# Transposes by DMA straight from SBUF, one per token tile, and zero matmuls before the first work, in a fused attention and FFN kernel

## The chip, the cores and the metric

The kernel runs on one core of a Trainium2 chip. The metric is the device time of one execution in microseconds (us). Profiles show one profiled execution; their span runs from the first to the last instruction. The engines in them are PE (TensorE matmuls), PEld (TensorE weight loads), DVE (VectorE), ACT (ScalarE), POOL (GpSimd) and SP (SyncE, which here only issues DMAs; SPq is its queue).

## What is computed

The input x has 2048 tokens of 1024 features. LayerNorm gives xn; a linear attention block (32 heads of 32) and a SwiGLU FFN with hidden size 3584 both work on xn. Cut to what matters:

```python
xn = layernorm(x)
q, k, v = split_heads(xn @ wqkv)                   # 32 heads of 32
phi = lambda t: where(t > 0, t + 1, exp(t)) + 1e-6
kv, z = einsum(phi(k), v), sum(phi(k))             # over all tokens
o = (phi(q) @ kv) / (phi(q) . z + 1e-6)
s = o @ wo
g = silu((silu(xn @ w_gate) * (xn @ w_up)) @ w_down)
out = x + s * g
```

All inputs and the output are bfloat16.

## The kernel before

TensorE multiplies along the partition axis, so it needs xn and o with features on partitions and tokens on the free axis (`xnT`, `oT`), while LayerNorm and the attention's division produce them with tokens on partitions (`xn`, `o_blk`). The 2048 tokens are 16 tiles of 128 (`NT`), in 4 blocks (`NB`) of 4 tiles (`TPB`). Phase 1 goes over the 16 token tiles: LayerNorm, transpose, then four groups (`c` = 0 to 3) of eight matmuls each, two for k and two for v (`emit_Bmm`, evacuated by `emit_Bev`), and the sum over tokens of k times v (`emit_C`, tile `kvz`). Phase 2 makes q, divides (`emit_ND`), transposes o (`emit_OT`) and multiplies by wo (`emit_S`). Phase 3 is the FFN, which uses a Strassen-like scheme with sums of xn (`S`) and of weights (`T`). Engines execute in the order in which the program emits, except where noted.

LayerNorm of tile i: statistics on VectorE, 1/sqrt by Newton steps on small tiles on GpSimd, the normalization on VectorE. Two tiles (0 and 1) take the root from ScalarE instead.

```python
def emit_stats(i):                       # VectorE: bn_stats x2, bn_aggr
    ...
def emit_rstd(gid):
    eng = nc.gpsimd
    ...
    eng.tensor_scalar(out=a[:, 0:n], in0=mv[:, 0:n, 1], scalar1=EPS_LN, scalar2=None, op0=ALU.add)
    nc.vector.tensor_single_scalar(out=yi, ...)          # first guess by the bits
    nc.vector.tensor_scalar(out=yi, ...)
    for _ in range(3):                                   # NR_ITERS
        eng.tensor_tensor(out=w[:, 0:n], in0=y, in1=y, op=ALU.mult)
        eng.tensor_tensor(out=w[:, 0:n], in0=w[:, 0:n], in1=a[:, 0:n], op=ALU.mult)
        eng.tensor_scalar(out=w[:, 0:n], in0=w[:, 0:n], scalar1=-0.5, scalar2=1.5, ...)
        eng.tensor_tensor(out=y, in0=y, in1=w[:, 0:n], op=ALU.mult)
def emit_N(i):                           # VectorE: xn = (x - mean) * rstd
    xn = work.tile([P, D], BF16, name="xn", tag="xn")    # pool of 2
    ...
```

Tiles 0 to 7 are transposed on TensorE, eight 128x128 transposes each, and copied out of PSUM. Tiles 8 to 15 go, four at a time, to DRAM and come back through a transposing DMA:

```python
def emit_TR(i):                          # tiles 0 to 7
    tr_ps = psC.tile([P, dch, P], BF16, name="tr_ps", tag="C")
    for dc in range(dch):
        nc.tensor.transpose(tr_ps[:, dc, :], xn[:, ...], ident[:])
    ...                                  # copy to xnT by VectorE (tiles 0, 1) or ScalarE

def emit_A2_block(b):                    # tiles 8 to 15
    xn_blk = work.tile([P, TPB, D], BF16, name="xn_blk", tag="xn_blk")
    for t in range(TPB):
        emit_norm(b * TPB + t, xn_blk[:, t, :])
    nc.sync.dma_start(out=blk_rows_pt(xn_dram, b), in_=xn_blk[:])
    nc.sync.dma_start_transpose(out=xn_blk_tiles[b][:], in_=blk_rows(xn_dram, b))
```

The evacuation of a k group (`emit_phi`, not in place for the first nine tiles) is two ScalarE passes, exp into `e_t` and relu into `r_t`, and two VectorE passes, which write `pk_sb`. `e_t` and `r_t` have two buffers each, the kv PSUM tiles three. The main loop of phase 1:

```python
for i in range(2, NT):
    for c in range(NCH):                                 # 4
        emit_Bmm(i, c)
        if c == 0:
            if i + 1 < NPE:                              # NPE = 8
                emit_TR(i + 1)
            emit_C(i - 1)
        emit_Bev(i, c)
        ...                                              # norms and statistics of later tiles
    if i == 3 or i == 5:
        wt, wv = (wq_sb, wqkv_v) if i == 3 else (wo_sb, wo_v)
        for c in range(NCC):
            nc.gpsimd.dma_start(out=wt[:, :, c * CW:(c + 1) * CW], in_=wv[:, :, c * CW:(c + 1) * CW])
    if i >= 10:
        prep(1)                                          # weight sums T for the FFN, on GpSimd
```

In phase 2 each half block of o (two token tiles) goes to DRAM and back:

```python
def emit_OT(b, hf):
    ...
    nc.sync.dma_start(out=rows.rearrange("(t p) d -> p t d", p=P), in_=o_blk[:, hf * th:(hf + 1) * th, :])
    nc.sync.dma_start_transpose(out=oT_tiles[b][:, :, hf * tk:(hf + 1) * tk], in_=rows)

def nd_item(b, t):
    def f():
        emit_ND(b, t)
        if t % 2 == 1:
            emit_OT(b, t // 2)
            prep(1)
    return f
```

In the last block the four `emit_ND` stand among the `emit_S` of the block before it; then come the sums `S` for the FFN (`emit_Ssum`, VectorE, into memory that the o blocks have left) and the eight `emit_S` of the last block. The loads of the first FFN weights are held back until the first of those eight begins.

Of the kernel before, what the change touches and what calls it, by code (L numbers as in the profile page):

```python
# [10 lines left out]
ALU = mybir.AluOpType  # L11
# [10 lines left out]
def kernel(  # L22
# [11 lines left out]
    nc = tc.nc  # L34
# [22 lines left out]
    NJ = (G + GPT - 1) // GPT  # L57
    EPS_LN = 1e-5
    EPS = 1e-6
    PE_T_BLOCKS = min(2, NB)  # L60
    NPREP = 12

    wqkv_v = A_wqkv.rearrange("(dc p) n -> p dc n", p=P)
# [41 lines left out]
    def xn_ap(dcs, tok):  # L105
        b = tok.start // TB
        return xn_blk_tiles[b][:, dcs, tok.start - b * TB:tok.stop - b * TB]
# [7 lines left out]
        nc.gpsimd.memset(v_bufs[k][:, :, P:P + 1], 1.0)  # L115
    KVZ = late.tile([P, G, NDW], BF16, name="KVZ")
    s_dram = dram.tile([S, D], BF16, name="s_dram")
    xn_dram = dram.tile([S, D], BF16, name="xn_dram")
    o_dram = dram.tile([S, D], BF16, name="o_dram")
    HK = DC // 2  # L120
    TB2 = 2 * TB
    t_drams = {}

    def blk_rows(t_dram, b):
        return t_dram[b * TB:(b + 1) * TB, :]

    def blk_rows_pt(t_dram, b):
        return t_dram[b * TB:(b + 1) * TB, :].rearrange("(t p) d -> p t d", p=P)

    def emit_phi(work, t_ps, dst, W, in_place=False, act=False):  # L130
        e_t = work.tile([P, W], FP32, name="e_t", tag="e_t")
# [123 lines left out]
    with ExitStack() as p1:  # L255
        wpool = p1.enter_context(tc.tile_pool(name="p1w", bufs=1))
        work = p1.enter_context(tc.tile_pool(name="p1work", bufs=2))
        small = p1.enter_context(tc.tile_pool(name="p1small", bufs=4))

        wkv_sb = wpool.tile([P, DC, 2 * D], BF16, name="wkv_sb")  # L260

# [36 lines left out]
            load_wkv(c)  # L298
        for i in range(nx, NT):
            load_x(i)  # L300
        NPE = min(PE_T_BLOCKS * TPB, NT)
        STAT_AT = {2: (8, 9), 3: (10, 11), 5: (12, 13), 6: (14, 15)}
        FMAX = nc.vector.BN_STATS_FMAX
        SCH = min(FMAX, D)
        NSC = D // SCH
# [4 lines left out]
        grp_state = {}  # L310

        def grp_of(i):
            return i if i < NPE else NPE - PE_T_BLOCKS + i // TPB

        def grp_tiles(gid):
            if gid < NPE:
                return [gid]
            b = gid - NPE + PE_T_BLOCKS
            return list(range(b * TPB, min((b + 1) * TPB, NT)))

        def emit_stats(i):
            gid = grp_of(i)
            if gid not in grp_state:
                mv = small.tile([P, TPB, AGG], FP32, name="mv", tag="mv")
                rstd = small.tile([P, TPB], FP32, name="rstd", tag="rstd")
                grp_state[gid] = (mv, rstd, grp_tiles(gid))
            mv, rstd, tiles = grp_state[gid]
            k = tiles.index(i)
            stats = small.tile([P, NSC, nc.vector.BN_STATS_DIM], FP32, name="stats", tag="stats")
            xr = x_ap(i).rearrange("p (c f) -> p c f", f=SCH)  # L330
            sts = [nc.vector.bn_stats(out=stats[:, c, :], in_=xr[:, c, :]) for c in range(NSC)]
# [13 lines left out]
            nc.vector.reciprocal(out=rstd[:, 0:n], in_=rstd[:, 0:n])  # L345
            return sq

        def emit_rstd(gid):
            eng = nc.gpsimd
            mv, rstd, tiles = grp_state[gid]  # L350
            n = len(tiles)
            a = small.tile([P, TPB], FP32, name="lna", tag="lna")
            eng.tensor_scalar(out=a[:, 0:n], in0=mv[:, 0:n, 1], scalar1=EPS_LN, scalar2=None, op0=ALU.add)
# [12 lines left out]
        def emit_norm(i, dst, cols=None):  # L366
            mv, rstd, k = ln_state[i]
            src = x_ap(i) if cols is None else x_ap(i)[:, cols]
            return nc.vector.tensor_scalar(out=dst, in0=src, scalar1=mv[:, k, 0:1], scalar2=rstd[:, k:k + 1],
                                           op0=ALU.subtract, op1=ALU.mult)  # L370
# [1 line left out]
        xn_tiles = {}  # L372

        def emit_N(i):
            xn = work.tile([P, D], BF16, name="xn", tag="xn")
            xn_tiles[i] = xn
            if i == 0:
                for hh in range(2):
                    cols = slice(hh * (D // 2), (hh + 1) * (D // 2))
                    emit_norm(i, xn[:, cols], cols=cols)  # L380
            else:
                emit_norm(i, xn[:])
            ln_state.pop(i)

        def emit_TR(i):
            tok = slice(i * P, (i + 1) * P)
# [3 lines left out]
            for hh in range(nh):  # L390
# [5 lines left out]
                    nc.vector.tensor_copy(out=dst, in_=tr_ps[:])  # L396
                else:
                    nc.scalar.copy(out=dst, in_=tr_ps[:])

        def emit_A2_block(b):  # L400
            xn_blk = work.tile([P, TPB, D], BF16, name="xn_blk", tag="xn_blk")
            for t in range(TPB):
                emit_norm(b * TPB + t, xn_blk[:, t, :])
                ln_state.pop(b * TPB + t)
            nc.sync.dma_start(out=blk_rows_pt(xn_dram, b), in_=xn_blk[:])
            nc.sync.dma_start_transpose(out=xn_blk_tiles[b][:], in_=blk_rows(xn_dram, b))

        pkv_tiles = {}

# [2 lines left out]
        def emit_Bmm(i, c):  # L412
            tok = slice(i * P, (i + 1) * P)
            kv_ps = psB.tile([P, CW], FP32, name="kv_ps", tag="B")
            kv_banks[(i, c)] = kv_ps
            for dc in range(DC):
                mm = nc.tensor.matmul(kv_ps[:], lhsT=xn_ap(dc, tok), rhs=wkv_sb[:, dc, c * CW:(c + 1) * CW],  # L417
                                      start=(dc == 0), stop=(dc == DC - 1))
                if dc == 0 and c == 0:
                    marks[("B", i)] = mm  # L420
# [23 lines left out]
        def ln_pre(i):  # L444
            emit_stats(i)
            emit_rstd(grp_of(i))

        emit_stats(0)
        emit_rstd_act(0)
        emit_N(0)  # L450
# [3 lines left out]
        emit_N(1)  # L454
        emit_Bmm(0, 0)
        emit_TR(1)
        ln_pre(2)
        emit_Bev(0, 0)
        emit_Bmm(0, 1)
        emit_Bmm(1, 0)  # L460
        emit_Bev(0, 1)
        ln_pre(3)
        emit_Bev(1, 0)
        emit_N(2)
        emit_Bmm(1, 1)
        emit_Bmm(0, 2)
        emit_Bev(1, 1)
        emit_Bev(0, 2)
        emit_Bmm(1, 2)
        emit_Bev(1, 2)  # L470
        ln_pre(4)
        emit_TR(2)
        emit_N(3)
        emit_Bmm(0, 3)
        emit_Bev(0, 3)
        emit_Bmm(1, 3)
# [2 lines left out]
        for i in range(2, NT):  # L479
            for c in range(NCH):  # L480
                emit_Bmm(i, c)
                if c == 0:
                    if i + 1 < NPE:
                        emit_TR(i + 1)
                    emit_C(i - 1)
                emit_Bev(i, c)
                if c == 1:
                    if i + 2 < NPE:
                        emit_N(i + 2)
                    if 5 <= i + 3 < NPE:  # L490
                        ln_pre(i + 3)
                if c == 2:
                    if i in STAT_AT:
                        for k in STAT_AT[i]:
                            emit_stats(k)
                            if k % TPB == TPB - 1:
                                emit_rstd(grp_of(k))
                    if i - 1 in STAT_AT and STAT_AT[i - 1][-1] % TPB == TPB - 1:
                        emit_A2_block(STAT_AT[i - 1][-1] // TPB)
            if i == 3 or i == 5:  # L500
                wt, wv = (wq_sb, wqkv_v) if i == 3 else (wo_sb, wo_v)
                for c in range(NCC):
                    nc.gpsimd.dma_start(out=wt[:, :, c * CW:(c + 1) * CW], in_=wv[:, :, c * CW:(c + 1) * CW])
            if i >= 10:
                prep(1)
        emit_C(NT - 1)
        ps1.close()
# [36 lines left out]
    with ExitStack() as p2:  # L544
# [35 lines left out]
                    in1=rden[:, 0:ng, :, None].to_broadcast([P, ng, HPG, DH]),  # L580
                    op=ALU.mult)

        def emit_OT(b, hf):
            if hf == 0:
                oT_tiles[b] = otp.tile([P, G, TB], BF16, name="oT", tag="oT")
            o_blk = o_blks[b]
            th, tk = TPB // 2, TB // 2
            rows = o_dram[b * TB + hf * tk:b * TB + (hf + 1) * tk, :]
            nc.sync.dma_start(out=rows.rearrange("(t p) d -> p t d", p=P), in_=o_blk[:, hf * th:(hf + 1) * th, :])
            nc.sync.dma_start_transpose(out=oT_tiles[b][:, :, hf * tk:(hf + 1) * tk], in_=rows)  # L590

        def emit_S(b, t, cc):
            oT = oT_tiles[b]
# [20 lines left out]
        def nd_item(b, t):  # L614
            def f():
                emit_ND(b, t)
                if t % 2 == 1:
                    emit_OT(b, t // 2)
                    prep(1)
            return f  # L620

# [239 lines left out]
```

## Time and profile before

| | |
|---|---|
| median of 3 runs | 815.3 us |
| lowest and highest | 811.02, 815.36 us |
| span of the profiled execution | 813.0 us |
| TensorE busy | 792.4 us |
| VectorE, ScalarE, GpSimd busy | 446.0, 236.9, 205.0 us |
| DMA | 178.92 MB, mean 220 GB/s |

Phase 1 lasts until about 135 us, phase 2 until about 261 us, the FFN until the end. In the profile an operation is named by its line, engine, output and inputs; `tr_ps` are the TensorE transposes, `kv_ps` the matmuls for k and v, `kvz` the sum over tokens, `q_ps` and `s_ps` those of phase 2, `yb`, `xb`, `zw`, `y_pd` and `y_ps` the FFN. `a <- b` in a list of waits means that a waited for b. Overlapping matmuls are shown with their whole length through the pipeline, so the rate of a series is read from the length of the series, not from the mean of one.

### The profile page before, as it was taken

To read this page: it belongs to the slowest core of one execution; us is meant where nothing else is said; L and a number is where in the kernel's file an instruction comes from. 1 tells how busy PE (TensorE), PEld (TensorE's weight loads), DVE (VectorE), ACT (ScalarE), POOL (GpSimd) and SP (SyncE) were. 2 spreads that over 40 slices of the span, in tenths; PEclk is the share of its full clock that TensorE was granted. 3 is DMA by queue.
4 is the path that set the end of the run, shared out by engine and by line. 5 is a ranking of instruction groups with operands and counts; after the bars stand their busy time and mean duration, and the time that the engine had idled before them with its cause. 6 is when DMAs were issued, how large, how long until landed. Compare 5 with 4: busy or idle time off the path is not lost.

```text
span 813.0 us, 10086 instructions
## 1 busy us (share of the span) xinstructions
PE 792.4 (97%) x3808; PEld 432.4 (53%) x3808; DVE 446.0 (55%) x700; ACT 236.9 (29%) x388; POOL 205.0 (25%) x309
## 2 busy tenths in 40 slices
PE   6999999999989999999999999999999999999997
PEld 2544444444444666666665444466666666644443
DVE  6676334684544666767765044177667676610405
ACT  4544333866523322222221020032222222200102
POOL 2472695034342253443650010010000000000200
PEclk9999999999998999999999999999999999999999
DMA  9239953079689778778686548489777777753641
GB/s 318 97 135 232 299 215 156 0 228 262 222 255 296 237 228 264 244 232 276 205 302 216 189 137 322 136 275 323 255 258 249 238 251 253 258 195 130 218 144 52
DMA packets 150784, 178.92 MB, mean 220 GB/s; under 512 B 30928, under 2 KB 106064, under 8 KB 150736
## 3 DMA queue, kind: packets, MB, share of 16 engines
q1 hardware_dynamic: 137984, 137.25, 53.7%
q0 software_dynamic: 10304, 36.71, 12.7%
q10 hardware_dynamic: 2448, 4.33, 1.6%
q8 instruction: 30, 0.49, 0.3%
q14 instruction: 18, 0.15, 0.1%
HBM read 127.93 MB, written 44.04 MB: 212 GB/s over the span
## 4 chain that ended last, share of the span: by engine, by line
PE 88%; DMA 5%; DVE 3%; POOL 2%; issue 1%; ACT 1%; SPq 0%; DVEq 0%
PE zw L663 25%; PE xb L663 12%; PE y_pd L748 12%; PE y_ps L748 11%; PE kv_ps L417 8%; PE s_ps L600 7%; PE yb L663 6%; PE q_ps L165 4%; DMA oT<-o_dram 2%; DMA xnT<-xn_dram 1%; DMA xn_dram<-xn_blk 1%; DMA xp<-in_A_x_dram 1%; PE kvz L439 1%; PE nd_ps L569 1%; DVE sy L785 0%
## 5 line engine op out<-in xcount | busy, mean ns | idle before, releaser
L663 PE MATMUL zw<-S,T 128*128 128x512 f32 x672 | 175.3, 409 | 0.0
L748 PEld LDWEIGHTS <-hT 128*128 128x128 bf16 x896 | 87.7, 98 | 105.7
L663 PEld LDWEIGHTS zw<-S,T 128*128 128x128 f32 x672 | 126.4, 188 | 32.3
L417 PE MATMUL kv_ps<-wkv_sb,xnT 128*128 128x512 bf16 x512 | 115.2, 383 | 1.9 <-DMA xnT<-xn_dram 1.8
L663 PE MATMUL xb<-xnT,w_sb 128*128 128x512 bf16 x448 | 115.2, 380 | 0.0
L748 PE MATMUL y_ps<-w_sb,hT 128*128 128x512 bf16 x448 | 103.2, 379 | 0.0
L748 PE MATMUL y_pd<-w_sb,hT 128*128 128x512 bf16 x448 | 102.9, 379 | 0.0
L663 PEld LDWEIGHTS <-w_sb 128*128 128x128 bf16 x672 | 56.8, 98 | 83.1 <-issue 30.5
L785 DVE TENSOR_TENSOR sy<-sy,io 128x512 f32<-128x512 f32 (+1 forms) x33 | 22.2, 671 | 137.6 <-ACT sy L784 137.4
L788 POOL DMA_DIRECT2D out_dram<-io x24 | 13.0, 541 | 332.6 <-DVE io L786 332.6
L417 PEld LDWEIGHTS <-xnT 128*128 128x128 bf16 x512 | 49.6, 98 | 59.6 <-DMA xnT<-xn_dram 2.3
L682 ACT COPY s<-xb 128x512 f32<-128x512 f32 x56 | 32.7, 584 | 158.4 <-PE xb L663 158.4
L221 POOL TENSOR_TENSOR T<-w_sb 128x512 fp32r<-128x512 bf16 x28 | 32.5, 1161 | 175.1 <-DMA w_sb<-in_B_w_gate_dram 80.2
L683 DVE TENSOR_TENSOR s<-yb,s 128x512 f32<-128x512 f32 x56 | 38.6, 689 | 63.9 <-ACT s L682 63.9
L663 PE MATMUL yb<-S,T 128*128 128x512 f32 x224 | 71.5, 441 | 0.0
L600 PE MATMUL s_ps<-wo_sb,oT 128*128 128x512 bf16 x256 | 60.1, 389 | 5.1 <-DMA oT<-o_dram 5.1
L165 PE MATMUL q_ps<-xnT,wq_sb 128*128 128x512 bf16 x256 | 58.2, 379 | 0.0
L720 ACT ACTIVATE sg<-sg 128x1024 f32<-128x1024 f32 x28 | 29.6, 1058 | 97.6 <-DVE sg L716 97.6
L663 PE MATMUL zw<-S,w_sb 128*128 128x512 f16 x224 | 58.0, 382 | 0.0
L784 ACT ACTIVATE sy<-y_pd 128x512 f32<-128x512 f32 x16 | 8.7, 594 | 159.9 <-PE y_pd L748 159.9
L684 DVE TENSOR_TENSOR s<-zw,s 128x512 f32<-128x512 f32 x56 | 38.7, 692 | 26.6 <-PE zw L663 26.5
L726 DVE TENSOR_TENSOR hT<-cu,sg 128x1536 bf16<-128x1536 f32 x28 | 49.9, 1781 | 0.0
(80 smaller groups left out, 794.1 us busy)
## 6 DMA issues: line engine op xcount, KB each, us to landing
w_sb<-in_B_w_down_dram SPq DMA_DIRECT2D x56, 512.0 KB, 4.1
T<-t_g SPq DMA_DIRECT2D x52, 512.0 KB, 4.4
w_sb<-in_B_w_gate_dram SPq DMA_DIRECT2D x40, 512.0 KB, 4.8
t_g<-T POOLq DMA_DIRECT2D x28, 512.0 KB, 4.9
w_sb<-in_B_w_up_dram SPq DMA_DIRECT2D x28, 512.0 KB, 6.6
t_u<-T POOLq DMA_DIRECT2D x28, 512.0 KB, 5.6
T<-t_u SPq DMA_DIRECT2D x28, 512.0 KB, 4.8
o_dram<-o_blk SPq DMA_DIRECT2D x8, 512.0 KB, 4.8
```

What stands on the lines that cost most here:

```text
L165: nc.tensor.matmul(q_ps[:], lhsT=wq_sb[:, dc, g * P:(g + 1) * P], rhs=xn_ap(dc, btok), start=(dc == 0), stop=(dc == DC - 1))
L221: nc.gpsimd.tensor_tensor(out=T1, in0=b12, in1=b11, op=ALU.subtract)
L417: mm = nc.tensor.matmul(kv_ps[:], lhsT=xn_ap(dc, tok), rhs=wkv_sb[:, dc, c * CW:(c + 1) * CW], start=(dc == 0), stop=(dc == DC - 1))
L600: mm = nc.tensor.matmul(s_ps[:], lhsT=oT[:, c, ttok], rhs=wo_sb[:, c, cc * CW:(cc + 1) * CW], start=(c == 0), stop=(c == G - 1))
L663: nc.tensor.matmul(out, lhsT=lhs(k), rhs=rhs(k), start=(first and k == 0), stop=(k == HK - 1), skip_group_check=True)
L682: nc.scalar.copy(out=s1[:], in_=x_[:])
L683: nc.vector.tensor_tensor(out=s2[:], in0=y_[:], in1=s1[:], op=ALU.add)
L684: nc.vector.tensor_tensor(out=s3[:], in0=zw[:, 0, :], in1=s2[:], op=ALU.add)
L720: nc.scalar.activation(out=c[:, 1:3, :], in_=c[:, 1:3, :], func=ACT.Silu)
L726: nc.vector.tensor_tensor(out=hv[:, TB:4 * TB], in0=c[:, 1:4, :].rearrange("p a b -> p (a b)"), in1=sg[:, 1:4, :].rearrange("p a b -> p (a ...
L748: nc.tensor.matmul(ys[(t, c)], lhsT=h[:, fc, tt], rhs=wt[:, o:o + CW], start=(fc == 0), stop=(fc == FC - 1), skip_group_check=True)
L785: nc.vector.tensor_tensor(out=sy[:], in0=sy[:], in1=s_in[:, cs], op=ALU.mult)
```

## The change

Tiles 4 to 15 of xn and all of o are transposed by a DMA that reads SBUF and writes SBUF, one per token tile, right after the tile is made; the copies in DRAM are gone. TensorE transposes only tiles 0 to 3. LayerNorm works tile by tile on a new schedule (`PRE_AT`): statistics and root of one or two tiles per token tile, the normalization one token tile later. The add in front of the Newton steps moves to VectorE, and tile 2 takes the whole root on VectorE. `xn` has four buffers. Eleven matmuls of zeros run on TensorE while x is loaded, meant to have its clock up when the first real matmul comes. The loads of wq and wo move from GpSimd's queue to SP's, a quarter after each of tiles 3 to 6, and the weight sums start at tile 8 instead of 10.

```diff
-    PE_T_BLOCKS = min(2, NB)
+    NPE = 4
+    NWARM = 11
...
-    xn_dram = dram.tile([S, D], BF16, name="xn_dram")
-    o_dram = dram.tile([S, D], BF16, name="o_dram")
...
+        xnw = p1.enter_context(tc.tile_pool(name="p1xn", bufs=4))
-        small = p1.enter_context(tc.tile_pool(name="p1small", bufs=4))
+        small = p1.enter_context(tc.tile_pool(name="p1small", bufs=6))
...
-        STAT_AT = {2: (8, 9), 3: (10, 11), 5: (12, 13), 6: (14, 15)}
+        PRE_AT = {2: (5, 6), 3: (7, 8), 4: (9, 10), 5: (11, 12), 6: (13, 14), 7: (15,)}
...
-        def emit_rstd(gid):
-            eng = nc.gpsimd
+        def emit_rstd(gid, eng=None):
+            eng = eng or nc.gpsimd
...
-            eng.tensor_scalar(out=a[:, 0:n], ...)
+            nc.vector.tensor_scalar(out=a[:, 0:n], ...)
...
         def emit_N(i):
-            xn = work.tile([P, D], BF16, name="xn", tag="xn")
+            xn = xnw.tile([P, D], BF16, name="xn", tag="xn")
...
+            if i >= NPE:
+                xn_tiles.pop(i)
+                nc.sync.dma_start_transpose(out=xn_ap(slice(0, DC), slice(i * P, (i + 1) * P)), in_=xn[:])
...
-        def emit_A2_block(b):
-            ...
+        warm = work.tile([P, CW], BF16, name="warm", tag="warm")
+        nc.vector.memset(warm[:], 0.0)
+        wps = psB.tile([P, CW], FP32, name="warm_ps", tag="B")
+        for k in range(NWARM):
+            nc.tensor.matmul(wps[:], lhsT=warm[:, 0:P], rhs=warm[:], start=True, stop=True)
         emit_stats(0)
...
-        ln_pre(2)
+        ln_pre(2, nc.vector)
         emit_Bev(0, 0)
         emit_Bmm(0, 1)
+        emit_N(2)
         emit_Bmm(1, 0)
         emit_Bev(0, 1)
         ln_pre(3)
         emit_Bev(1, 0)
-        emit_N(2)
...
         emit_Bev(1, 2)
+        emit_N(3)
         ln_pre(4)
         emit_TR(2)
-        emit_N(3)
...
-                if c == 1:
-                    ...
-                if c == 2:
-                    ...
-            if i == 3 or i == 5:
-                ...
-                    nc.gpsimd.dma_start(out=wt[:, :, c * CW:(c + 1) * CW], in_=wv[:, :, c * CW:(c + 1) * CW])
-            if i >= 10:
+                if c % 2 == 1:
+                    for k in (PRE_AT[i - 1] if i - 1 in PRE_AT else (4,) if i == 2 else ())[c // 2:c // 2 + 1]:
+                        emit_N(k)
+                    for k in PRE_AT.get(i, ())[c // 2:c // 2 + 1]:
+                        ln_pre(k)
+            if 3 <= i < 7:
+                wt, wv = (wq_sb, wqkv_v) if i < 5 else (wo_sb, wo_v)
+                c = (i - 3) % 2
+                nc.sync.dma_start(out=wt[:, :, c * CW:(c + 1) * CW], in_=wv[:, :, c * CW:(c + 1) * CW])
+            if i >= 8:
                 prep(1)
...
-        def emit_OT(b, hf):
-            if hf == 0:
+        def emit_OT(b, t):
+            if t == 0:
                 oT_tiles[b] = otp.tile([P, G, TB], BF16, name="oT", tag="oT")
-            o_blk = o_blks[b]
-            ...
-            nc.sync.dma_start(out=rows.rearrange("(t p) d -> p t d", p=P), in_=o_blk[:, hf * th:(hf + 1) * th, :])
-            nc.sync.dma_start_transpose(out=oT_tiles[b][:, :, hf * tk:(hf + 1) * tk], in_=rows)
+            nc.sync.dma_start_transpose(out=oT_tiles[b][:, :, t * P:(t + 1) * P], in_=o_blks[b][:, t, :])
...
                 emit_ND(b, t)
+                emit_OT(b, t)
                 if t % 2 == 1:
-                    emit_OT(b, t // 2)
                     prep(1)
```

More of the change, by code (lines that the diff above doesn't have):

```diff
@@ L122 @@
     t_drams = {}
[L124 to L128, printed above, removed]
     def emit_phi(work, t_ps, dst, W, in_place=False, act=False):
@@ L300 @@
             load_x(i)
-        NPE = min(PE_T_BLOCKS * TPB, NT)
-        STAT_AT = {2: (8, 9), 3: (10, 11), 5: (12, 13), 6: (14, 15)}
+        PRE_AT = {2: (5, 6), 3: (7, 8), 4: (9, 10), 5: (11, 12), 6: (13, 14), 7: (15,)}
         FMAX = nc.vector.BN_STATS_FMAX
@@ L312, in grp_of @@
         def grp_of(i):
-            return i if i < NPE else NPE - PE_T_BLOCKS + i // TPB
+            return i
         def grp_tiles(gid):
[L316 to L319, printed above, removed]
+            return [gid]
         def emit_stats(i):
@@ L352, in emit_rstd @@
             a = small.tile([P, TPB], FP32, name="lna", tag="lna")
-            eng.tensor_scalar(out=a[:, 0:n], in0=mv[:, 0:n, 1], scalar1=EPS_LN, scalar2=None, op0=ALU.add)
+            nc.vector.tensor_scalar(out=a[:, 0:n], in0=mv[:, 0:n, 1], scalar1=EPS_LN, scalar2=None, op0=ALU.add)
             yi = rstd[:, 0:n].bitcast(I32)
@@ L398, in emit_TR @@
                     nc.scalar.copy(out=dst, in_=tr_ps[:])
-        def emit_A2_block(b):
[L401 to L406, printed above, removed]
         pkv_tiles = {}
@@ L442, in emit_C, with ln_pre @@
                                  skip_group_check=True)
-        def ln_pre(i):
+        def ln_pre(i, eng=None):
             emit_stats(i)
-            emit_rstd(grp_of(i))
+            emit_rstd(grp_of(i), eng)
+        warm = work.tile([P, CW], BF16, name="warm", tag="warm")
[3 more added lines that the diff above has]
+            nc.tensor.matmul(wps[:], lhsT=warm[:, 0:P], rhs=warm[:], start=True, stop=True)
         emit_stats(0)
@@ L486 @@
                 emit_Bev(i, c)
-                if c == 1:
[L488 to L491, printed above, removed]
-                if c == 2:
[L493 to L499, printed above, removed]
-            if i == 3 or i == 5:
-                wt, wv = (wq_sb, wqkv_v) if i == 3 else (wo_sb, wo_v)
-                for c in range(NCC):
-                    nc.gpsimd.dma_start(out=wt[:, :, c * CW:(c + 1) * CW], in_=wv[:, :, c * CW:(c + 1) * CW])
-            if i >= 10:
+                if c % 2 == 1:
[8 more added lines that the diff above has]
+            if i >= 8:
                 prep(1)
@@ L581, in emit_ND @@
                     op=ALU.mult)
-        def emit_OT(b, hf):
-            if hf == 0:
+        def emit_OT(b, t):
+            if t == 0:
                 oT_tiles[b] = otp.tile([P, G, TB], BF16, name="oT", tag="oT")
-            o_blk = o_blks[b]
-            th, tk = TPB // 2, TB // 2
-            rows = o_dram[b * TB + hf * tk:b * TB + (hf + 1) * tk, :]
-            nc.sync.dma_start(out=rows.rearrange("(t p) d -> p t d", p=P), in_=o_blk[:, hf * th:(hf + 1) * th, :])
-            nc.sync.dma_start_transpose(out=oT_tiles[b][:, :, hf * tk:(hf + 1) * tk], in_=rows)
+            nc.sync.dma_start_transpose(out=oT_tiles[b][:, :, t * P:(t + 1) * P], in_=o_blks[b][:, t, :])
         def emit_S(b, t, cc):
```

## The prediction

> **What bounds the kernel now.** I read the page first (busy shares, slices, DMA issues), then the waits of TensorE, the chain of waits, the timeline of each engine over the first 290 us, and a table of short windows. The page:
>
> ```profile
> span 813.0 us, 10086 instructions
> ...
> PE 792.4 (97%) x3808; PEld 432.4 (53%) x3808; DVE 446.0 (55%) x700; ACT 236.9 (29%) x388; POOL 205.0 (25%) x309
> ...
> oT<-o_dram SPq DMA_TRANSPOSE x8, 4.7
> ...
> xnT<-xn_dram SPq DMA_TRANSPOSE x2, 8.9
> ```
>
> TensorE is the bound: it is idle for 813.0 - 792.4 = 20.6 us. The last two lines, from the DMA view, are the transposes that the change replaces, with the median us from issue to landing. Next, everything TensorE waits for:
>
> ```profile
> PE tr_ps L393 <- DVE xn L369: 8.5, 4, 5.9
> PE s_ps L600 <- DMA oT<-o_dram: 5.1, 2, 4.7
> PE kv_ps L417 <- DMA xnT<-xn_dram: 1.8, 1, 1.8
> PE kvz L439 <- ACT v_sb L432: 0.4, 1, 0.4
> ```
>
> Columns: total us, times, longest. They sum to 15.8 us; the timeline shows that the remaining 4.7 us is the tail after the last matmul (from 808.3 to 813.0), which the change does not touch. The first line splits in the TensorE timeline into 5.91 us at the start, 0.27 (token tile 1), 0.83 (tile 2) and 1.47 (tile 7). The chain of waits shows the DMA round trips in front of two of these gaps: each is a store to DRAM followed by a transposing load.
>
> ```profile
> 55.63 7.83 DMA xn_dram<-xn_blk
> 63.48 11.78 DMA xnT<-xn_dram
> ...
> 236.77 8.07 DMA oT<-o_dram
> 244.89 16.09 PE s_ps L600 x64
> ```
>
> Columns: start, length, what. The last line carries a second cost. In warm stretches 32 matmuls of this kind take 6.91 us in the chain, 0.216 us each; 64 should take 13.8 us and took 16.09. The windows around it say why (length; busy time of PE, PEld, DVE, ACT, POOL; granted clock; DMA share; GB/s):
>
> ```profile
> 241.00:247.00 6.00, 2.11 (x6) 0.74 (x7) 0.00 (x0) 0.00 (x0) 0.00 (x0) 0.61 0.97 250
> 247.00:252.00 5.00, 5.00 (x20) 2.09 (x19) 4.75 (x3) 2.97 (x3) 0.00 (x0) 0.78 0.65 142
> 252.00:257.00 5.00, 5.00 (x25) 2.27 (x24) 4.24 (x2) 1.76 (x3) 1.00 (x1) 1.00 1.16 332
> ```
>
> After 4.65 us idle the clock fell and took until about 250 us to come back. So this one late transpose costs 4.65 + (16.09 - 13.8) = 6.9 us, the largest single item.
>
> [...] the first eight kv matmuls take 3.45 us in the timeline (0.43 each, against 0.216 warm), and the gap of 4.65 us is followed by a clock of 0.61 to 0.78, while gaps of 1.5 and 1.8 us leave 1.00. [...] In the queue's waits SP stands 33.0 us in 8 waits on the o store before its transposes, and 11.2 us in 2 on the xn store. A transpose from SBUF has no such wait. [...] The trace has them only from DRAM: 512 KB in 4.2 to 8.1 us. No run here shows one from SBUF. [...] the small rstd operations on GpSimd take 0.19 us, and 0.65 to 0.72 us beside pk_sb and xn work of VectorE.
>
> **The change, part by part.** All of it lies in the first 245 us; the 540 us of FFN after it stay as they are, with no TensorE gap to remove.
>
> *TensorE transposes.* Tiles 4 to 7 go from TensorE to DMA. A set of eight takes 0.45 us on TensorE (tr_ps at 34.77, the next work at 35.22): 4 x 0.45 = 1.8 us off the bound. With tile 7's transpose goes its wait of 1.47 us.
>
> *xn by DMA, per tile.* The block of four behind one store and one transpose becomes four transposes of 256 KB. New order: statistics of tile k two to eight tiles ahead of use, norm one tile-time later, transpose at once. By the new order tile 4 is normed in tile 2, at about 31 us by my walk through the VectorE queue, and TensorE reaches it at about 40 us. A 512 KB transpose lands in 4.2 us without much traffic, so I estimate 3 to 4 us for 256 KB: 4 or 5 us to spare, and more for every later tile. The wait of 1.83 us goes.
>
> *o by DMA, per tile.* Tile 0 of the last block has its o at 229.2 us (VectorE timeline), its transpose can land at about 233, and its s_ps matmuls are due at 240.24. The 4.65 us, the 2.3 us of slow clock and the 0.41 us of block 0 go: 7.4 us. What follows must not become late in turn: the S sums of the FFN (four VectorE operations, 9.1 us, from 247.22 to 256.24) can begin when the o blocks have been read, at about 241 instead of 247, and the FFN would begin at 240.2 + 13.8 = 254: they end about 250. This slack is 4 us, enough.
>
> *Zero matmuls.* Eleven at 0.43 us are 4.7 us of cold running, from about 1.3 us (the memset now stands third in VectorE's order) to about 6.0 us; the first real transpose is at 5.91. So the eight cold matmuls become warm and save 1.7 us of busy time. But TensorE then stands at the transpose of tile 1, whose norm ends at 10.73 because x tile 1 lands at 8.06 us. That wait is 0.27 us now and would be about 1.9. I count 0.
>
> *Start order.* Tile 2's rstd moves to VectorE (twelve operations near 0.19 us, 2.3 us) and its norm ahead of other work: at about 18 us instead of 20.8. But pk_sb of tile 0 comes two us later, holds ScalarE and, through a PSUM bank, about 0.6 us of TensorE. I count half the 0.83 us: 0.4.
>
> *What is added.* Two tiles of LayerNorm per token tile in tiles 3 to 6. On VectorE, from the timeline at 32.03: norm, statistics, aggregate and three small ones are 2.6 us, two are 5.1; the phi of pk_sb is 2.4: 7.5 us against a TensorE tile of 16 x 0.432 + 0.46 = 7.4. On GpSimd a chain of twelve rstd operations takes 3.3 us free and up to 5.4 (53.86 to 59.21) beside VectorE; two of 4.2 are 8.4 us. Both are slightly over the pace for four tiles. Walking the queues, norms wait one to two us for rstd, pk_sb slips, and kvz of tile 7 waits about 1 us. I count 1 us lost.
>
> Sum: 1.8 (TensorE transposes) + 1.5 (tile 7) + 1.8 (xn block) + 0.4 (o, block 0) + 6.9 (o, last block) + 0.4 (tile 2) = 12.8, minus 1.0 for LayerNorm: 11.8 us, 1.4%. From 815.3: 803.5.
>
> **Rivals.** (A) *LayerNorm becomes the bound in tiles 3 to 8.* For it: the sums of 7.5 and 8.4 against 7.4 above; [...] a chain can be nearer 4.9, and my walk then gives stalls of 2 to 2.5 us in three or four tiles, some 7 us. Against it: pk_sb has some 3 us before kvz needs it, the load drops after tile 6, and the add of each chain has moved to VectorE. It would make 808 to 810. (B) *Transposes from SBUF are slow, or collect on the SP queue behind each other and the wq and wo loads that now share it.* For it: nothing measured from SBUF, and the two 1 MB transposes of before kept the SP queue for 9.59 and 3.91 us. Against it: from DRAM 512 KB needs as little as 1.31 us of SP, and only 256 KB per 3.7 us is asked for. At 8 us each the xn chain would fall behind at tiles 4 to 6[...]: 815 to 835. (C) *The gain is larger:* the warm start counts in full, tile 2 is free, nothing is lost in LayerNorm. Tile 1 speaks against the first. All items with the whole warm start come to about 12.8 + 1.7 + 0.4 + 0.3 = 15.2 us, 800.1. So more than 2% (below 799.0) needs something that I do not see.
>
> **Range and chances.** Before, the runs spread from 811.0 to 815.4, so 4 us of the early waits come and go. Full success is 800, the middle 803.5, rival A 808 to 810: 799.5 to 809 for 8 in 10. Over 2% faster is at the edge of what there is to gain: 7%. Over 2% slower needs rival B in full: 5%.
>
> **What would show it.** Right: TensorE waits for DMA at s_ps near zero; granted clock 1.00 from the start of the last s_ps to the FFN; its 64 matmuls in 13.8 us; the FFN's first matmul about 11 to 12 us earlier than 260.6; kv at 0.216 us from its first matmul on, with a wait of about 2 us for tile 1. Wrong: waits of kvz or kv_ps on VectorE work in tiles 5 to 9 (A), DMA transposes over 6 us from issue to landing and waits of kv_ps on xnT (B), a new wait at the first FFN matmul, or gaps in the FFN that were not there.

## The result and the profile after

The changed kernel takes 801.6 us in the median of 4 runs (801.25 to 804.99) against 814.4 for the kernel before beside it; the ratio is 0.986, with a 95% interval of 0.982 to 0.990. A later set of runs gave 803.4 against 814.6, ratio 0.9862 (0.9829 to 0.9895). So 11 to 13 us came off, within the predicted range.

The page of the profiled execution, first its head, then the DMA view:

```profile
span 799.1 us, 10159 instructions
...
PE 790.2 (99%) x3787; PEld 431.3 (54%) x3787; DVE 453.0 (57%) x739; ACT 232.9 (29%) x384; POOL 215.5 (27%) x357
...
oT<-o_blk SPq DMA_TRANSPOSE x16, 3.2
xnT<-xn SPq DMA_TRANSPOSE x12, 3.2
```

TensorE's idle time fell from 20.6 to 799.1 - 790.2 = 8.9 us. A transpose of 256 KB from SBUF lands 3.2 us after its issue in the median. What TensorE still waits for (total us, times, longest):

```profile
PE tr_ps L386 <- DVE xn L359: 1.6, 2, 1.1
PE warm_ps L437 <- DVE warm L434: 1.3, 1, 1.3
PE kv_ps L402 <- ACT r_t L139: 0.5, 1, 0.5
PE kvz L424 <- ACT v_sb L417: 0.4, 1, 0.4
PE kv_ps L402 <- DVE xnT L389: 0.2, 1, 0.2
```

No DMA is left in this list, neither `xnT` nor `oT`. The two places where the chain of waits of the kernel before showed a transpose are now matmuls alone (start, length, what):

```profile
226.17 20.72 PE s_ps L578 x96
246.89 0.94 PE yb L641 x4
```

All 96 matmuls run at 20.72 / 96 = 0.216 us, and the first FFN matmul (`yb`) follows at once. To see where the 13.9 us between the two spans (813.0 and 799.1) came from, compare when TensorE reaches the same piece of work, read off its timeline in both traces:

| start on TensorE of | before | after | lead | gained here |
|---|---|---|---|---|
| kvz of tile 0 | 24.77 | 23.63 | 1.14 | 1.14 |
| kvz of tile 3 | 43.03 | 41.00 | 2.03 | 0.89 |
| kvz of tile 7 | 77.04 | 70.47 | 6.57 | 4.54 |
| kvz of tile 8 | 84.41 | 77.83 | 6.58 | 0.0 |
| first q_ps | 135.32 | 128.74 | 6.58 | 0.0 |
| first s_ps | 171.03 | 163.88 | 7.15 | 0.57 |
| last 64 s_ps | 244.89 | 232.92 | 11.97 | 4.82 |
| first yb | 260.63 | 246.54 | 14.09 | 2.12 |

(232.92 is worked out: the series of 96 begins at 226.01 in the timeline, and 32 of it take 6.91.) Up to kvz of tile 7 there are four sets of transposes (1.8 in all), the wait of tile 7 (1.47) and, in front of the kv matmuls of tile 8, the wait for the xn block (2.0, the lead from kvz of tile 6, 4.57, to that of tile 7, 6.57); the last two rows are the gap at the last block of o and the slow clock behind it.

### The profile page after: what moved, and what is told of

Its sections match the earlier page's. It is cut to its first block, busy times and chain, and to the rows that moved or that the text cites. A ratio compares the mean times of both kernels' runs of the same rounds, so it can differ in the third digit from the quotient of the medians.

```text
span 799.1 us, 10159 instructions
## 1 busy us (share of the span) xinstructions
PE 790.2 (99%) x3787; PEld 431.3 (54%) x3787; DVE 453.0 (57%) x739; ACT 232.9 (29%) x384; POOL 215.5 (27%) x357
## 4 chain that ended last, share of the span: by engine, by line
PE 96%; DVE 2%; ACT 0%; DMA 0%; issue 0%; DVEq 0%; ACTq 0%
PE zw L641 26%; PE kv_ps L402 13%; PE xb L641 12%; PE y_pd L726 12%; PE y_ps L726 11%; PE s_ps L578 7%; PE q_ps L158 7%; PE yb L641 7%; PE nd_ps L551 1%; PE kvz L424 1%; DVE sy L763 1%; DVE stats L321 0%; DVE io L764 0%; DMA xp<-in_A_x_dram 0%; PE tr_ps L386 0%
## 5 line engine op out<-in xcount | busy, mean ns | idle before, releaser
L402 PE MATMUL kv_ps<-wkv_sb,xnT 128*128 128x512 bf16 x512 | 113.6, 379 | 0.7 <-ACT r_t L139 0.5
L578 PE MATMUL s_ps<-wo_sb,oT 128*128 128x512 bf16 x256 | 57.8, 379 | 0.0
```

Source lines behind the costliest of these rows:

```text
L578: mm = nc.tensor.matmul(s_ps[:], lhsT=oT[:, c, ttok], rhs=wo_sb[:, c, cc * CW:(cc + 1) * CW], start=(c == 0), stop=(c == G - 1))
```

## Experiments

"Before" and "changed" name the two kernels. In the edits, `+` is what the experiment has.

**1. o alone, zero matmuls alone, all but the zero matmuls.** First, which part of the change brings how much.

o_only is the kernel before with

```diff
-    dma_start(out=o_dram rows, in_=o_blk half); dma_start_transpose(out=oT half, in_=o_dram rows)
+    dma_start_transpose(out=oT_tiles[b][:, :, t * P:(t + 1) * P], in_=o_blks[b][:, t, :])
```

> The kernel before with only the o part: one DMA transpose from SBUF per token tile, no copy in DRAM. Theory (each item of the sum stands by itself): the waits of s_ps on oT go (0.4 + 4.65 us) and the 64 s_ps matmuls of the last block take 13.8 us instead of 16.1: 7.3 us faster than before, near 807, and the first FFN matmul at about 253.3 us instead of 260.6. Rival (the FFN's sums S and weight sums T were hidden behind that wait and now end it): TensorE waits for S or T at its first yb or zw matmul, and the gain is under 5 us.

warm_only is the kernel before with

```diff
+    warm = KVZ[:].rearrange("p g n -> p (g n)")[:, 0:CW]; nc.vector.memset(warm, 0.0)
+    for k in range(11): nc.tensor.matmul(wps[:], lhsT=warm[:, 0:P], rhs=warm, ...)
     emit_stats(0)
```

> The kernel before with only the eleven zero matmuls (their operand is zeroed in a tile that is not yet in use). Theory of the prediction (TensorE then stands for x tile 1): the first eight kv matmuls take 1.7 us instead of 3.45, the transposes of tile 1 still start at 10.8 us, and the time stays within 0.5 us of before. Rival (x tile 1 is not what holds tile 1, or arrives earlier): the transposes of tile 1 start about 0.8 us earlier, as in the changed kernel (10.02 us), and the time is about 1 us lower.

no_warm is the changed kernel with the eleven matmuls and their memset deleted.

> The changed kernel without the zero matmuls. Theory of the prediction (zero matmuls give nothing): the same time as the changed kernel within 0.5 us, about 801.6. Rival (they carry the 1.1 us by which the changed kernel is ahead at its first kvz, 23.63 against 24.77 us): about 1 us slower, first kvz at about 24.7 us, tile 1 transposed at about 10.8 us.

| | us, median (lowest to highest) | ratio to before, 95% |
|---|---|---|
| before | 814.4 (810.9 to 819.0) | |
| o_only | 807.8 (806.4 to 811.9) | 0.992 (0.9887 to 0.9952) |
| warm_only | 810.7 (807.6 to 814.2) | 0.9956 (0.9936 to 0.9976) |
| no_warm | 802.3 (801.5 to 802.7) | 0.9844 (0.9815 to 0.9874) |

o alone brings 6.6 us, and in its trace TensorE waits for neither `S` nor `T` ahead of the FFN. The changed kernel loses nothing measurable without the zero matmuls. But warm_only is faster than before by 3.7 us, which doesn't fit; its trace, of the fastest of its fifteen executions (807.6 us), says what else differs. In it the wait at the last half blocks of o is only 0.72 us, though nothing was done to o, and its first eight kv matmuls take 1.90 instead of 3.47 us, as meant. So the 4.65 us gap isn't there in every execution of the same road through DRAM. Experiment 3 takes this up.

For the zero matmuls, the timelines of six traces answer directly: TensorE begins the transposes of tile 1 0.60 us after VectorE begins that tile's normalization, which hangs on x tile 1.

| | norm of tile 1 | transposes of tile 1 | kvz of tile 0 |
|---|---|---|---|
| before | 10.18 | 10.78 | 24.77 |
| warm_only | 9.65 | 10.25 | 24.24 |
| changed | 9.42 | 10.02 | 23.63 |
| no_warm | 10.32 | 10.92 | 24.64 |
| all_dram (below; with zero matmuls) | 10.36 | 10.96 | 24.56 |
| after_again (below; with zero matmuls) | 11.14 | 11.74 | 26.42 |

no_warm and all_dram have x tile 1 at the same time, one without and one with zero matmuls: 24.64 and 24.56. The zero matmuls are worth 0.1 us there. Measured from the norm, kvz of tile 0 comes 14.59 us later before and 14.21 in the changed kernel: 0.38 us. The new order takes away the wait of tile 2 (0.83 us) and brings one of 0.45 us, of `kv_ps` for `r_t`. The other 0.76 us of the first row of the milestones is x tile 1 that happened to land earlier (10.18 - 9.42). In after_again kvz of tile 0 comes 15.28 us after the norm: behind its wait of 2.33 us for tile 1 the granted clock fell, as its table of windows shows:

```profile
13.00:15.00 2.00, 2.00 (x6) 0.72 (x5) 1.86 (x7) 0.30 (x1) 0.00 (x0) 0.50 1.09 358
```

So there TensorE was at full pace at 7 us behind the zero matmuls (its first four kv matmuls take 1.04 us in the timeline, where the first eight before take 3.47; the granted clock reads 1.00 for those too, so the pace alone shows it), and slower again behind the wait: the 40 kv matmuls from 12.20 take 10.48 us, against 8.80 for 40 before. Over all twelve experiments and both kernels that norm begins between 9.27 and 11.92 us.

**2. Is it the clock?** before_fill is the kernel before with twelve zero matmuls into a free PSUM tile in front of the last block's second-to-last group of s_ps.

```diff
+        for k in range(12):
+            nc.tensor.matmul(fill_ps[:], lhsT=zero[:, 0:P], rhs=zero[:], start=True, stop=True)
```

> The kernel before with twelve zero matmuls (2.6 us) ahead of the s_ps matmuls of the last block, in the gap in which TensorE waits 4.65 us for oT. Nothing else moves. Theory (the 2.3 us by which these 64 matmuls are slow are the clock[...]): the gap left is about 2 us, the granted clock stays 1.00, the 64 matmuls take 13.8 us, and the time is 2.3 us lower than before although the matmuls still start when oT lands, near 245 us. Rival (they are slow for another reason, such as the transposes of the second half arriving late): the 64 matmuls still take about 16 us and the time does not change.

TensorE's timeline in before_fill, at the gap (start, length; in brackets the idle time before and what ended it):

```profile
242.56 2.75 PE L650 MATMUL fill_ps<-zero 128*128 128x512 bf16 x11
246.89 13.99 PE L602 MATMUL s_ps<-wo_sb,oT 128*128 128x512 bf16 x63 [1.57 <-DMA oT<-o_dram]
```

and the stretch from 240 us in its table of windows (the number after the last bracket is the clock):

```profile
240.00:245.00 5.00, 4.95 (x24) 2.22 (x23) 0.00 (x0) 1.17 (x2) 0.00 (x0) 1.00 1.08 289
245.00:250.00 5.00, 3.43 (x17) 1.45 (x16) 1.42 (x1) 1.35 (x1) 0.00 (x0) 1.00 0.54 205
```

The transpose is as late as before, 2.75 + 1.57 = 4.3 us, but the clock stays at 1.00 and the last s_ps take 13.99 instead of 16.09 us. The 2.1 us behind the gap are the clock, as the prediction had it. In the times this is 813.25 against 814.39, ratio 0.9982 (0.9966 to 0.9998): 1.1 us in the medians, half of the 2.3 expected. The gap isn't there in every execution, as warm_only showed.

**3. Why is the transpose of o late?** The changed kernel also starts GpSimd's weight sums two tiles earlier; each ends with 1 MB stored to DRAM from GpSimd's queue. Their last stores ahead of the FFN begin at 226.31 and 236.33 us before, but at 184.87 and 197.42 in the changed kernel. The second of before's comes beside the transpose that is late (timeline of all engines):

```profile
236.33 1.10 POOL L229 DMA_DIRECT2D t_u<-T  x2
...
236.77 4.30 SPq L590 DMA_TRANSPOSE oT<-o_dram  x1
```

So there are two theories for the gap: the road through DRAM itself, or its meeting with such a store. o_as_before is the changed kernel with o through DRAM:

```diff
-    dma_start_transpose(out=oT_tiles[b][:, :, t * P:(t + 1) * P], in_=o_blks[b][:, t, :])
+    dma_start(out=o_dram rows, in_=o_blk half); dma_start_transpose(out=oT half, in_=o_dram rows)
```

> The changed kernel with o again written to DRAM in half blocks and transposed from there, xn and the zero matmuls as changed. Theory 1 (the DRAM round trip of the last half block is itself late): TensorE waits about 4 to 5 us at the last block's s_ps and loses another 2 us to the slower clock after it, so 808 to 809 us. Theory 2 (the wait came from a collision with GpSimd's last two 1 MB weight-sum stores, which the changed kernel has finished by 200 us): a wait under 1.5 us, and within 2 us of the changed kernel.

prep_early is the kernel before with the weight sums early and nothing else:

```diff
-            if i >= 10:
+            if i >= 8:
                 prep(1)
```

> The kernel before with the weight sums of GpSimd begun two token tiles earlier, so that its stores are over before the last half block of o leaves; nothing else changed. Theory 2 (collision): the wait of 4.65 us before the last s_ps shrinks to under 1.5 us and the clock stays at 1.00, so 807 to 809 us. Theory 1 (the round trip itself): the wait stays above 3.5 us and the time within 2 us of the kernel before.

o_as_before takes 802.3 us (801.8 to 802.8; ratio 0.9851, 0.9830 to 0.9873): with o back on the road through DRAM nothing is lost. prep_early takes 808.1 (807.9 to 811.2; 0.9935, 0.9913 to 0.9957): with o untouched the gap is gone, and 6.5 us come off, as many as with o_only. The collision (theory 2) holds as the cause, the round trip by itself (theory 1) falls. Around the last block, the timelines of all engines show the store of o, its transpose and the s_ps, first in prep_early, then in o_as_before; no bracket means no wait:

```profile
234.80 0.38 SPq L589 DMA_DIRECT2D o_dram<-o_blk  x1
...
236.10 20.88 PE L600 MATMUL s_ps<-wo_sb,oT 128*128 128x512 bf16 x96
...
238.17 1.85 SPq L590 DMA_TRANSPOSE oT<-o_dram  x1
```

```profile
225.86 0.37 SPq L572 DMA_DIRECT2D o_dram<-o_blk  x1
...
227.16 4.05 PE L583 MATMUL s_ps<-wo_sb,oT 128*128 128x512 bf16 x18
...
228.91 2.17 SPq L573 DMA_TRANSPOSE oT<-o_dram  x1
```

To be sure, late_dram puts both back into the changed kernel: o as in o_as_before, and

```diff
-            if i >= 8:
+            if i >= 10:
                 prep(1)
```

> The changed kernel with o through DRAM in half blocks and GpSimd's weight sums begun at token tile 10, both as before; xn and the zero matmuls as changed. Theory 1 (o through DRAM and late stores of GpSimd must meet for the wait before the last s_ps to arise): the wait is back, up to 4.7 us with up to 2 us of slower clock behind it, 805 to 809 us. Theory 2 (the earlier end of the weight sums has nothing to do with it): within 1 us of the changed kernel.

Its timeline of all engines:

```profile
224.99 0.38 SPq L572 DMA_DIRECT2D o_dram<-o_blk  x1
...
229.07 2.59 SPq L573 DMA_TRANSPOSE oT<-o_dram  x1
229.31 1.10 POOL L223 DMA_DIRECT2D t_u<-T  x2
...
235.95 0.61 PE L583 MATMUL s_ps<-wo_sb,oT 128*128 128x512 bf16 x2 [2.61 <-DMA oT<-o_dram]
```

The gap is back, at 2.61 us. GpSimd issues its store (`t_u<-T`, two of 512 KB) 0.24 us after SP issues the transpose. The time is 805.2 us (804.3 to 810.4) beside 803.4 for the changed kernel (801.3 to 804.1) on the same chip; the intervals of the two ratios overlap, so it is the trace that shows the gap. The clock stayed at 1.00 (13.99 us for the last 64). In after_again it fell to 0.50 behind a gap of only 2.33 us. So in these traces the length of a gap alone does not tell whether the clock falls.

Side by side, in seven traces, the transpose of the half block from DRAM that TensorE needed soonest. "Allowed" is from the issue of the store of o to the moment that TensorE needs the half block (its start less its wait): 8.2 to 8.4 us in before, late_dram, prep_early and o_as_before.

| last block of o in | o stored | transposed | GpSimd's store | landed after | wait |
|---|---|---|---|---|---|
| before | 231.88 | 236.77 | 236.33 | 8.1 | 4.65 |
| before_fill | 234.37 | 238.52 | 238.37 | 8.3 | 4.3 |
| late_dram | 224.99 | 229.07 | 229.31 | 6.8 | 2.61 |
| all_dram, first block | 156.41 | 159.96 | 159.87 | 7.6 | 2.46 |
| warm_only | 230.55 | 234.54 | 236.88 | 4.3 | 0 |
| prep_early | 234.80 | 238.17 | none near | 4.2 | 0 |
| o_as_before | 225.86 | 228.91 | none near | 4.2 | 0 |

(warm_only's wait of 0.72 us is for the next half block.) In these seven rows, where GpSimd's 1 MB store is issued within half a microsecond of the transpose, the transpose takes 6.8 to 8.3 us to land; in the others 4.2 to 4.3. Those same seven traces hold 56 such transposes in all. The ten that have a store issued between 0.5 us before and 0.8 us after them land in 6.4 to 9.5 us; of the other 46, 43 land in 4.1 to 5.8 and three in 6.2 to 7.0. From the late transpose's issue at 236.77 in before to its landing, the only transfers issued beside that store are ScalarE's stores of s_sb and the next half block's store of o, and prep_early has these too.

Undisturbed, the road is 3.05 + 4.2 = 7.3 us for o_as_before, which fits into its 8.2 with 1 us to spare. In the kernel before it is 4.9 + 8.1 = 13.0 us, and 13.0 less the 8.36 allowed is the gap of 4.65. The first leg is longer too: GpSimd's store issued at 226.31 had not landed before 234.7, and the store of o beside it took 4.9 us instead of 3.05. Transposes from SBUF can be slow there as well: in the changed kernel the one issued at 167.0, beside a store at 167.28, took 7.3 us, as did the one at 176.6, behind a store at 174.26; nobody waited for either. Two others, at 184.0 and 196.57, with stores about 0.9 us behind them (184.87, 197.42), took 3.1. Whether the two share bandwidth or are held up in the DMA engines' queues was not tried.

**4. And xn: is it the missing DRAM copy?** all_dram is o_as_before with xn too through DRAM, but per token tile:

```diff
-    dma_start_transpose(out=xn_ap(..., tile i), in_=xn[:])
+    dma_start(out=xn_dram[i * P:(i + 1) * P, :], in_=xn[:])
+    dma_start_transpose(out=xn_ap(..., tile i), in_=xn_dram[i * P:(i + 1) * P, :])
```

> The changed kernel with both transposes fed from DRAM copies again: xn written and transposed per token tile, o per half block as before. Theory 1 (what the change brings comes from transposes off TensorE and from the earlier end of GpSimd's weight sums; the road through DRAM itself costs nothing so long as it starts early enough): within 1 us of the changed kernel. Theory 2 (the missing DRAM copies bring the gain): xn of some tile from 4 on arrives late, with a wait of 2 us or more at its kv matmuls, 804 us or more.

npe8 is the changed kernel with `NPE = 8`, and after_again the changed kernel itself, to stand beside them.

> The changed kernel with the transposes of token tiles 4 to 7 back on TensorE (tiles 8 to 15 and o by DMA as changed). Theory 1 (the change saved two separate things there: 4 x 0.45 us of transposes, and a wait of about 1.5 us at tile 7 that the re-ordered LayerNorm took away): 1.8 us slower than the changed kernel, without a wait at tile 7. Theory 2 (the wait was due to the transposes standing on TensorE): 3.3 us slower, with a wait for xn at tile 7.

> The changed kernel once more, to stand beside the other runs of this set on the same chip. All theories: within 1.5 us of its first time of 801.6 us.

| | us, median (lowest to highest) | ratio to before, 95% |
|---|---|---|
| after_again | 803.4 (801.3 to 804.1) | 0.9862 (0.9829 to 0.9895) |
| all_dram | 804.6 (802.8 to 806.6) | 0.9881 (0.9848 to 0.9915) |
| npe8 | 804.8 (802.8 to 807.5) | 0.9886 (0.9851 to 0.9921) |

all_dram is not told apart from after_again in the times (the intervals overlap). In its trace no tile of xn is late, kvz to kvz is 7.37 us from tile 1 to the end; its one new wait is that of the first block of o, with GpSimd's store beside the transpose (all engines):

```profile
159.87 1.10 POOL L224 DMA_DIRECT2D t_g<-T  x2
159.96 1.40 SPq L575 DMA_TRANSPOSE oT<-o_dram  x1
...
167.62 0.61 PE L585 MATMUL s_ps<-wo_sb,oT 128*128 128x512 bf16 x2 [2.46 <-DMA oT<-o_dram]
```

So for xn the first theory of this run holds (without its "within 1 us", 1.2 in the medians); for o the direct transpose is an insurance against such meetings. In npe8, TensorE's timeline at tile 7:

```profile
53.51 0.61 PE L386 MATMUL tr_ps<-ident,xn 128*128 128x128 bf16 x8
53.96 0.62 PE L424 MATMUL kvz<-v_sb,pk_sb 128*128 128x129 bf16 x8
54.42 7.07 PE L402 MATMUL kv_ps<-wkv_sb,xnT 128*128 128x512 bf16 x32
61.32 0.61 PE L386 MATMUL tr_ps<-ident,xn 128*128 128x128 bf16 x8
```

No bracket: the transposes wait for nothing, and the pace is 61.32 - 53.51 = 7.81 us against 7.37 without them. The 4 x 0.45 us are TensorE's transposes; the wait of 1.47 us at tile 7 is gone without moving them. In before, VectorE could not begin tile 7's norm until GpSimd's root chain for it had ended at 59.21 us; this chain began at 53.86, behind two loads of wq that GpSimd issued from 51.16 to 53.1. In npe8 that norm is done at 51.3, ten us ahead of its transposes. Both the new order of LayerNorm and the move of those loads to SP's queue can have done this; no run takes them apart. The 1.4 us in the medians agree in size, without being resolved.

**5. How near was rival A?** In the changed kernel GpSimd works without a pause from 34.5 to 77.8 us, and a pair of its root chains takes 7.75 us against TensorE's 7.37. From the changed kernel's timelines at tile 7, VectorE's write of the second half of pk_sb and TensorE's first load of that half as weights:

```profile
69.63 0.70 DVE L141 SCALAR_TENSOR_TENSOR pk_sb<-e_t,r_t 128x512 bf16<-128x512 f32 x1
...
70.64 0.10 PEld L424 LDWEIGHTS <-pk_sb 128*128 128x128 bf16 x1
```

VectorE is done with this half at 70.33. Where TensorE waits for it (newton4 below) the load follows 0.05 us later, so about 0.26 us are to spare here, after 1.40 at tile 4, 1.02 at tile 5 and 0.64 at tile 6. The 0.14 us of the expectation below runs to 70.47, where the kvz matmuls begin; those read the first half, done at 69.26. In after_again, where TensorE started later, tile 7 has 1.2 us to spare. To see the edge, newton4 adds one Newton step, four more small operations in each chain (and in tile 2's, on VectorE):

```diff
-        NR_ITERS = 3
+        NR_ITERS = 4
```

> The changed kernel with one more Newton step in each LayerNorm's rstd: four more GpSimd operations in each chain at about 0.27 us spacing, so a pair of chains takes about 9.8 us instead of 7.75, against 7.37 of a token tile on TensorE. Theory (GpSimd's chains have 0.14 us to spare at tile 7): TensorE waits 4 to 9 us in all for tiles 3 to 8, 806 to 812 us. Rival (LayerNorm has several us to spare): within 1 us of the changed kernel.

It takes 815.3 us (814.9 to 816.9; ratio 1.0013, 1.0001 to 1.0025): the whole gain is gone. Its waits of TensorE, and its timeline:

```profile
PE kvz L424 <- DVE pk_sb L141: 9.7, 9, 1.7
```

```profile
61.43 0.41 PE L424 MATMUL kvz<-v_sb,pk_sb 128*128 128x129 bf16 x4 [1.71 <-DVE pk_sb L141]
62.50 0.41 PE L424 MATMUL kvz<-v_sb,pk_sb 128*128 128x129 bf16 x4 [0.66 <-DVE pk_sb L141]
62.74 7.07 PE L402 MATMUL kv_ps<-wkv_sb,xnT 128*128 128x512 bf16 x32
71.53 0.40 PE L424 MATMUL kvz<-v_sb,pk_sb 128*128 128x129 bf16 x4 [1.72 <-DVE pk_sb L141]
```

TensorE's pace is now 71.53 - 61.43 = 10.1 us per tile, that of GpSimd's chains. The wait carries the name of VectorE's pk_sb, because in VectorE's timeline the writes of pk_sb stand behind norms that wait for GpSimd (ahead of kvz of tile 5 a norm at 57.70 after 1.90 us of waiting, then pk_sb at 60.69 and 61.75): VectorE's waits have one line in that stretch, with 14.6 us.

```profile
DVE xn L359 <- POOL rstd L354: 14.6, 10, 1.9
```

The theory held, but the expected 806 to 812 was too low: the pair of chains takes 10.1 us and not 9.8. The last kvz starts at 142.30 instead of 128.51, 13.8 us later: 9.7 are these waits, 0.9 one of `kv_ps`, 1.5 are lost up to kvz of tile 1, and some 1.7 remain, in series of matmuls that the waits break up. Rival A was real. It missed by 0.26 us in one execution and by 1.2 in another, and a small miss would have cost no more than the excess: in the changed kernel the chains lose only 7.75 - 7.37 = 0.38 us per tile.

**6. A try at the start.** x1_first is the changed kernel with x tile 1 loaded ahead of half of the first quarter of the weights:

```diff
     nc.sync.dma_start(out=wkv_sb[:, 0:hs, 0:CW], in_=wqkv_v[:, 0:hs, D:D + CW])
+    load_x(1)
     nc.sync.dma_start(out=wkv_sb[:, hs:DC, 0:CW], in_=wqkv_v[:, hs:DC, D:D + CW])
```

> The changed kernel with the load of x tile 1 issued ahead of the second half of the first quarter of the key and value weights. If tile 1's transposes wait for x tile 1 behind the weights: they start near 9.0 instead of 10.0 us, and the time is 0.5 to 1 us lower. Rival: the second half of that weight quarter then holds the first kv matmuls up by as much, and the time is within 0.5 us of the changed kernel.

803.2 us (802.4 to 804.3): nothing gained. TensorE now waits for the weights:

```profile
PE kv_ps L405 <- DMA wkv_sb<-in_A_wqkv_dram: 2.6, 2, 1.9
```

x tile 1 landed at 7.15 us, hardly before the 7.31 of the changed kernel, and the wait moved from tile 1 to the weights. No experiment is clearly faster than the changed kernel; no_warm has the lowest ratio, 0.9844, with an interval that takes in 0.986.

## Why the prediction was right, step by step

The total was right, 11.8 us predicted and 11 to 13 measured; two of its terms, 8.4 us together, had the right size for a wrong reason.

- *TensorE transposes, 1.8*: right. npe8 shows a pace of 7.81 against 7.37, 0.45 a tile.
- *Wait of tile 7, 1.5*: the size was right, the reason wrong. "With tile 7's transpose goes its wait" fails: npe8 keeps that transpose and has no wait. xn was late, behind GpSimd's root chain; that the same diff also cures this is luck for the sum.
- *xn block, 1.8*: about 2.0 measured; the prediction left open which of its differences (smaller pieces, earlier norm, no DRAM) did it. all_dram shows that leaving out DRAM isn't needed for it. A rival stays open: in before this transpose (63.48) lands after 11.8 us beside the 2 MB of wo that GpSimd began to load at 59.14, and the second block's, with no such load, after 5.9. With 5.9 it would have been in time for the 73.48 at which TensorE needed it. The change moves these loads to SP's queue; no run moves them alone.
- *o, last block, 6.9*: the size was right (4.82 + 2.12 in the milestones), and so was the clock (before_fill: 16.09 to 13.99). The cause was not. The "late transpose" was put down to the round trip as such, and SP's waits on the store of o (33.0 us in 8) were brought up for it. In the runs the undisturbed round trip (7.3 us) fits into the 8.2 to 8.4 allowed; it was late because GpSimd's 1 MB stores met both of its legs. The diff removes that in two ways, the transpose from SBUF and the earlier weight sums, and each alone suffices (o_only, prep_early). The prediction never costed the line `if i >= 8`. Had it laid GpSimd's stores beside SP's transposes in the timeline of before, 236.33 beside 236.77 would have stood out, and so would transposes that land in 4.2 us elsewhere.
- *o, first block, 0.4*: 0.57.
- *Tile 2, 0.4*: 0.38, once the arrival of x tile 1 is taken out, and by the two parts named: a wait of 0.83 us gone, one of 0.45 through ScalarE come.
- *Zero matmuls, 0*: right, and for the stated reason; the wait of tile 1 became 1.05 to 2.33 us in the traces with them (x1_first aside), around the "about 1.9" of the prediction. It left out that the clock can fall again behind such a wait, as it did in after_again (0.50 behind 2.33 us), at a cost of about 1 us (15.28 against 14.21).
- *LayerNorm, minus 1.0*: nothing was lost. The term was mis-sized: the pair of chains takes 7.75 us, not 8.4, and from tile 4 to tile 7 they fall behind by 3 x 0.38 = 1.1 us, out of a slack of 1.40. The prediction was right that the chains run just over the pace.
- *A sign of being wrong that came without harm*: two transposes of o took over 6 us to land, 7.3 each, beside or behind GpSimd's stores.

The sum by these measured terms is 1.8 + 1.47 + 2.0 + 0.57 + 6.9 + 0.4 = 13.1, without the term for LayerNorm; the 0.76 us of x tile 1's arrival in those two executions makes the 13.9 of the spans.

What stays open: why x tile 1's arrival differs by 2.6 us between executions, and why warm_only meets GpSimd's store more seldom than the kernel before, if it does. That the spread of the kernel before, 810 to 819 us, comes from such meetings fits the traces, but wasn't shown run by run.

## What to carry to other kernels

A gap with a DMA's name on it says which transfer was late, not why: compare that transfer's landing time with that of its siblings, and look at what other queues issued in the same microsecond, before you blame its road. When one diff changes both the road and the other traffic, undo each alone; here either was enough, and the simplest version is a change of one constant. And when several queues run near the pace of the engine that bounds the kernel, find the slack at each tile, not the mean busy share: GpSimd was 27% busy over the span, had 0.26 us to spare at tile 7, and four more small operations in each chain took the whole gain of 12 us.

## What was not expected of the hardware

- A DMA transpose of a half block from DRAM landed in 4.1 to 5.8 us in 43 of 46 cases, and in 6.4 to 9.5 us in all ten with 1 MB stored from another queue at nearly the same moment. From SBUF, 256 KB landed in 3.0 to 4.5 us in the changed kernel (median 3.2) but for two of 28, which took 7.3 us, one beside and one behind such a store.
- An idle gap of 4.65 us cost 2.1 us more by the clock (0.50 from 244.89 to 249 us in before), and 2.75 us of zero matmuls in a gap of 4.3 us saved all of that. One of 2.61 us left the clock at 1.00 (late_dram), but one of 2.33 us at the start was followed by 0.50 (after_again).
- Operations on 128x1 tiles, most of 0.19 us at a spacing of 0.27, were enough to hold TensorE up: with two chains of sixteen on GpSimd per token tile, 10.1 us, it fell to that pace for several tiles (newton4); with two chains of twelve, 7.75 us, it did not wait.
